# Weights by casting transfers, 1 KB runs of k and q, and eight chunks of pinned steps in an attention-and-feed-forward kernel

## The chip, the cores and the metric

The kernel runs on one core of one Trainium2 chip. The metric is the device time of one execution in microseconds (us). Runs e1 to e4, e5 to e8, e9 to e11, e12 to e14 and e15 with e16 are five sets of rounds on five chips, where the kernel before took 347.7 to 348.3 us; a difference between kernels of different sets is less sure by that much. A *profile* is one further look at one execution: its span is some 2 us shorter than the time.

Five engines matter. TensorE (PE in the profile, PEld for its weight loads) multiplies, VectorE is DVE, ScalarE is ACT, GpSimd is POOL, and SyncE (SP) issues most transfers. The transfers of all queues run on the same 16 DMA engines (the prediction names its source for this).

## The reference, cut to what matters

```python
# q, k, v: (8 batches, 8 heads, 576 tokens, 64), float32
scores = matmul(q, k.T) / 8                       # per batch and head
mask   = (rel >= 0) & (rel < 64)                  # each token sees itself and 63 before it
attn   = softmax(where(mask, scores, -1e9))
x      = matmul(attn, v) -> (4608 tokens, 512)    # heads side by side
h      = maximum(x @ w_in, 0)                     # w_in  (512, 2048)
out    = (h * h) @ w_out                          # w_out (2048, 512)
```

## The kernel before

It goes through the 4608 tokens in 36 chunks of 128 (two blocks of 64). Four chunks make a group of 512 tokens, so there are nine groups. For a chunk `i` there are four attention steps: `T` (transposes of k and q on TensorE), `S_` (scores, exp on ScalarE, mask on VectorE), `V` (values), `X` (transpose of the result). For the first eight chunks the feed-forward goes by chunk, in four quarters of w_in (`U` in what follows); from group 2 on it goes by whole groups. After the first eight chunks come the output products (`ops` in the profile), group by group, woven with the attention and feed-forward of later groups. A tile scheduler puts each engine's instructions in order, by the order of tracing and by what depends on what.

A block of 64 tokens needs the v of its own block and of the block before. `v_ev[i]` holds the v of chunk i. `v_od[i]` holds the block before on its upper half of partitions and chunk i's first block on its lower half, so each chunk copies its last block into the `v_od` of the next chunk (the carry). There are eight of each (`NV = 8`).

```python
    def load(i):
        sts = []
        for (src, nm) in ((k, "k"), (q, "q"), (v, "v")):
            st = stage.tile([P, H, D], FP32, name=f"{nm}_st", tag="st")
            ...                                       # runs of 256 B: 64 floats of one token and head
            nc.sync.dma_start(out=st[:], in_=src[b0, :, 64*j0:64*j0+P, :].rearrange("h p d -> p h d"))
            sts.append(st)
        ...                                           # k and q cast to 16 bits by GpSimd
        v_ev, v_od, v_next = v_evs[i % NV], v_ods[i % NV], v_ods[(i + 1) % NV]
        nc.gpsimd.tensor_copy(out=v_ev[:, :, 0:D], in_=sts[2][:])
        nc.gpsimd.tensor_copy(out=v_od[64:P, :, 0:D], in_=v_ev[0:64, :, 0:D])
        if i + 1 < NCK:
            nc.gpsimd.tensor_copy(out=v_next[0:64, :, 0:D], in_=v_ev[64:P, :, 0:D])   # the carry
    ...
    load(0)
    for s in load_w_in():      # 16 transfers of 256 KB from SyncE, each cast by VectorE
        s()
    NFIRST = 8
    for i in range(1, NV - 1): # chunks 1 to 6
        load(i)
    ...
    T(0), warm(6), S_(0), warm(6), V(0), warm(6), X(0), warm(4)   # chunk 0
    load(NV - 1)               # chunk 7, only now
    for s in load_w_out() + ffn_up_chunk(0):
        s()
    T(1), S_(1), warm(2), V(1), T(2), warm(2), X(1), S_(2)
    ...                        # the steps of chunks 1 to 7; loads of chunks 8 to 11; groups 0 to 8 of output
```

`warm(n)` issues n products of no use, meant to keep TensorE's clock up while it waits.

The softmax here doesn't subtract the row's maximum and nothing guards it: scores larger than these inputs give would overflow.

Of the kernel before, what the change touches and what calls it, by code (L numbers as in the profile page):

```python
# [9 lines left out]
FP32 = mybir.dt.float32  # L10
# [17 lines left out]
def kernel(  # L28
# [9 lines left out]
    nc = tc.nc  # L38
# [7 lines left out]
    W_SCALE = 100.0  # L46
    OUT_SCALE = 1.0 / (W_SCALE * W_SCALE)
# [6 lines left out]
    wst = ctx.enter_context(tc.tile_pool(name="wst", bufs=4))  # L54
# [11 lines left out]

    ident = const.tile([P, P], FP16, name="ident")
    make_identity(nc, ident[:])





    base = const.tile([P, 64], FP16, name="base")
# [23 lines left out]
    w_in_sb = const.tile([P, DMC, DFF], FP16, name="w_in_sb")  # L98
    w_out_sb = const.tile([P, FFC, DM], FP16, name="w_out_sb")

    NV = 8
    v_evs = [const.tile([P, H, 66], FP16, name=f"v_ev{i}") for i in range(NV)]
    v_ods = [const.tile([P, H, 66], FP16, name=f"v_od{i}") for i in range(NV)]
    for i in range(NV):
        nc.vector.memset(v_evs[i][:, :, 64:65], 1.0)
        nc.vector.memset(v_ods[i][:, :, 64:65], 1.0)
    nc.vector.memset(v_ods[0][0:64, :, 0:D], 0.0)

    def load_w_in():
        steps = []  # L110
        FQ = DFF // 4

        def one(quar, c):
            ws = wst.tile([P, FQ], FP32, name="ws", tag="ws")
            nc.sync.dma_start(out=ws[:], in_=moe_w_in[c * P:(c + 1) * P,  # L115
                                                      quar * FQ:(quar + 1) * FQ])
            nc.vector.tensor_scalar(  # L117
                out=w_in_sb[:, c, quar * FQ:(quar + 1) * FQ], in0=ws[:],
                scalar1=W_SCALE, scalar2=None, op0=ALU.mult)

        for quar in range(4):
            for c in range(DMC):
                steps.append(lambda quar=quar, c=c: one(quar, c))
        return steps

    def load_w_out():
        def one(f):
            ws = wst.tile([P, DM], FP32, name="ws2", tag="ws")
            nc.sync.dma_start(out=ws[:], in_=moe_w_out[f * P:(f + 1) * P, :])
            nc.gpsimd.tensor_copy(out=w_out_sb[:, f, :], in_=ws[:])  # L130

        return [lambda f=f: one(f) for f in range(FFC)]


# [7 lines left out]
    q16s, k16s, qTs, kTs, pms, xs = {}, {}, {}, {}, {}, {}  # L142

    def load(i):

        sts = []
        for (src, nm) in ((k, "k"), (q, "q"), (v, "v")):
            st = stage.tile([P, H, D], FP32, name=f"{nm}_st", tag="st")
            b0, j0 = divmod(2 * i, NB)
            if j0 + 1 < NB:  # L150
                nc.sync.dma_start(  # L151
                    out=st[:], in_=src[b0, :, 64 * j0:64 * j0 + P, :].rearrange("h p d -> p h d"))
            else:
                nc.sync.dma_start(
                    out=st[0:64], in_=src[b0, :, 64 * j0:S, :].rearrange("h p d -> p h d"))
                nc.sync.dma_start(
                    out=st[64:P], in_=src[b0 + 1, :, 0:64, :].rearrange("h p d -> p h d"))
            sts.append(st)
        k16s[i] = st16.tile([P, H * D], FP16, name="k16", tag="k16")
        nc.gpsimd.tensor_copy(out=k16s[i][:], in_=sts[0][:].rearrange("p h d -> p (h d)"))  # L160
        q16s[i] = st16.tile([P, H * D], FP16, name="q16", tag="q16")
        nc.gpsimd.tensor_copy(out=q16s[i][:], in_=sts[1][:].rearrange("p h d -> p (h d)"))
        v_ev, v_od, v_next = v_evs[i % NV], v_ods[i % NV], v_ods[(i + 1) % NV]
        nc.gpsimd.tensor_copy(out=v_ev[:, :, 0:D], in_=sts[2][:])
        nc.gpsimd.tensor_copy(out=v_od[64:P, :, 0:D], in_=v_ev[0:64, :, 0:D])
        if i + 1 < NCK:
            nc.gpsimd.tensor_copy(out=v_next[0:64, :, 0:D], in_=v_ev[64:P, :, 0:D])

    def transposes(i):
        ps = ps_att.tile([P, 2, HP, P], FP16, name="qkT_ps", tag="ps_a")  # L170
        for s, src in enumerate((k16s, q16s)):
            for hp in range(HP):
                nc.tensor.transpose(out=ps[:, s, hp, :], in_=src[i][:, hp * P:(hp + 1) * P],  # L173
                                    identity=ident[:])
        kT = attw.tile([P, HP, 192], FP16, name="kT", tag="kT")
        if i > 0:
            nc.vector.tensor_copy(out=kT[:, :, 0:64], in_=kTs[i - 1][:, :, P:192])
        else:
            nc.vector.memset(kT[:, :, 0:64], 0.0)
        nc.vector.tensor_copy(out=kT[:, :, 64:192], in_=ps[:, 0])  # L180
        qT = attw.tile([P, HP, P], FP16, name="qT", tag="qT")
        nc.scalar.activation(out=qT[:], in_=ps[:, 1], func=AF.Copy, scale=1.0)  # L182
        kTs[i], qTs[i] = kT, qT

    def scores(i):
        sc = [ps_att.tile([P, HP, 2, 64], FP32, name=f"sc{hh}", tag="ps_a") for hh in range(2)]
        for hp in range(HP):
            for blk in range(2):
                for hh in range(2):
                    r0 = 64 * hh  # L190
                    nc.tensor.matmul(  # L191
                        sc[hh][:, hp, blk, :], kTs[i][r0:r0 + 64, hp, 64 * blk:64 * blk + P],
                        qTs[i][r0:r0 + 64, hp, 64 * blk:64 * blk + 64], start=True, stop=True)
        j0 = 2 * i % NB
        mask = mask_first if j0 == 0 else mask_second if j0 + 1 == NB else mask_inner
        pms[i] = []
        for hh in range(2):
            pm = attw.tile([P, HP, 2, 64], FP16, name=f"pm{hh}", tag=f"pm{hh}")
            nc.scalar.activation(out=pm[:], in_=sc[hh][:], func=AF.Exp,
                                 scale=1.0 / float(D) ** 0.5)  # L200
            nc.vector.tensor_tensor(out=pm[:], in0=pm[:], in1=mask, op=ALU.min)
            pms[i].append(pm)
# [40 lines left out]

    def ffn_up(g):
        h2s[g] = h2pool.tile([P, FFC, 512], FP16, name="h2", tag="h2")

        def one(f):
            hps = ps_up.tile([P, 512], FP32, name="hps", tag="ps_u")
            for c in range(DMC):
                nc.tensor.matmul(  # L250
                    hps[:], w_in_sb[:, c, f * P:(f + 1) * P], xT_of(g)[:, c, :],
                    start=(c == 0), stop=(c == DMC - 1))
            hrelu = hrp.tile([P, 512], FP32, name="hrelu", tag="hrelu")
            nc.scalar.activation(out=hrelu[:], in_=hps[:], func=AF.Relu)  # L254
            nc.vector.scalar_tensor_tensor(  # L255
                out=h2s[g][:, f, :], in0=hps[:], scalar=0.0, in1=hrelu[:],
                op0=ALU.max, op1=ALU.mult)
# [3 lines left out]
    def ffn_up_chunk(i):  # L261

        g, t0 = i // 4, i % 4 * P
        if g not in h2s:
            h2s[g] = h2pool.tile([P, FFC, 512], FP16, name="h2", tag="h2")

        def one(fq):
            hps = ps_up.tile([P, 4, P], FP32, name="hps4", tag="ps_u")
            for f in range(4):
                for c in range(DMC):  # L270
                    nc.tensor.matmul(  # L271
                        hps[:, f, :], w_in_sb[:, c, (4 * fq + f) * P:(4 * fq + f + 1) * P],
                        xT_of(g)[:, c, t0:t0 + P], start=(c == 0), stop=(c == DMC - 1))
            hrelu = hrp.tile([P, 4, P], FP32, name="hrelu4", tag="hrelu")
            nc.scalar.activation(out=hrelu[:], in_=hps[:], func=AF.Relu)
            nc.vector.scalar_tensor_tensor(  # L276
                out=h2s[g][:, 4 * fq:4 * fq + 4, t0:t0 + P], in0=hps[:], scalar=0.0,
                in1=hrelu[:], op0=ALU.max, op1=ALU.mult)

        return [lambda fq=fq: one(fq) for fq in range(FFC // 4)]  # L280
# [8 lines left out]
    def ffn_out(g):  # L289
        hold = {}  # L290

        def one(ts, fq):
            if fq == 0:
                hold["ps"] = ps_out.tile([P, DM], FP32, name="ops", tag="ps_o")
            for f in range(4 * fq, 4 * fq + 4):
                nc.tensor.matmul(  # L296
                    hold["ps"][:], h2s[g][:, f, ts * P:(ts + 1) * P], w_out_sb[:, f, :],
                    start=(f == 0), stop=(f == FFC - 1))
# [9 lines left out]



    load(0)
    for s in load_w_in():
        s()
    NFIRST = 8
    for i in range(1, NV - 1):
        load(i)
    T, S_, V, X = [lambda i, fn=fn: fn(i) if i < NFIRST else None
                   for fn in (transposes, scores, values, to_xT)]
    T(0), warm(6), S_(0), warm(6), V(0), warm(6), X(0), warm(4)
    load(NV - 1)  # L320
    for s in load_w_out() + ffn_up_chunk(0):
        s()
    T(1), S_(1), warm(2), V(1), T(2), warm(2), X(1), S_(2)
    for i in range(1, NFIRST):
        up = ffn_up_chunk(i)
        up[0](), V(i + 1), T(i + 2), up[1](), up[2](), X(i + 1), S_(i + 2), up[3]()
# [42 lines left out]
```

## Time and profile before

| | before |
|---|---|
| time, median of 4 runs | 348.03 us (347.95 to 348.61) |
| span of the profile | 345.9 us |
| TensorE busy | 324.3 us (94%) |
| first feed-forward product | 19.4 us |
| w_in complete on the core | 25.6 us |
| end of the first eight chunks | 75.4 us |

The page's table of engines, its slices (each digit is the busy share of a fortieth of the span, in tenths), and the start of its chain of the work that ended last, kernel before:

```profile
span 345.9 us, 7917 instructions
...
PE 324.3 (94%) x3146; PEld 178.2 (52%) x3146; DVE 207.9 (60%) x506; ACT 163.8 (47%) x289; POOL 121.5 (35%) x204
...
PE   1957888999999999999999999999999999999995
...
GB/s 200 249 252 239 234 247 252 207 230 228 243 172 61 93 121 123 121 124 155 212 185 182 170 135 184 185 87 27 23 45 36 30 32 32 30 30 32 35 88 62
...
PE 83%; DVE 7%; DMA 5%; ACT 2%; SPq 1%; issue 1%; ACTq 0%
```

TensorE is at nine tenths or more from the eighth slice on (60 us), and without a gap from about 75 us. What can be gained lies before that. The timeline of TensorE shows the feed-forward of chunk 0: start and duration in us, then the line and the operation, then the idle time ahead of it and who ended that.

```profile
19.41 1.05 PE L271 MATMUL hps_446<-xT,w_in_sb 128*128 128x128 f16 x16 [0.98 <-DVE xT L226]
...
22.17 1.05 PE L271 MATMUL hps_486<-xT,w_in_sb 128*128 128x128 f16 x16 [0.82 <-DVE h_397 L276]
...
25.63 0.90 PE L271 MATMUL hps_506<-xT,w_in_sb 128*128 128x128 f16 x13 [1.62 <-DVE w_in_sb L117]
```

The last quarter of w_in holds TensorE until 25.6 us: the weights pass one by one through SyncE's transfers and VectorE's casts, as the group of these casts shows (16 of them, 438 ns each; 12.2 us of VectorE's idle time ended by their transfers):

```profile
L117 DVE TENSOR_SCALAR w_in_sb<-ws 128x512 f16<-128x512 f32 x16 | 7.0, 438 | 12.2 <-DMA ws<-in_moe_w_in_dram 12.1
```

The table of windows for 25 to 35 us gives the rest of the loss: the granted clock (the column PEclk, after the five busy columns) is 0.64 and 0.68 of full speed there.

```profile
25.00:30.00 5.00, 2.67 (x49) 2.11 (x49) 3.93 (x9) 1.62 (x3) 3.75 (x6) 0.64 1.03 232
30.00:35.00 5.00, 4.70 (x60) 3.77 (x58) 2.55 (x7) 2.14 (x5) 4.62 (x9) 0.68 0.99 224
```

The dense work of TensorE, estimated from the durations in this trace (the prediction has the sum), is about 317 us, so about 29 us are lost, nearly all before 75 us.

### The profile page before, as it was taken

Reading aid. Unit: us, or ns where it says so; the run is one execution under the profiler, and the core shown is the slowest. Engines: PE = TensorE matmul, PEld = TensorE weight load, DVE = VectorE, ACT = ScalarE, POOL = GpSimd, SP = SyncE. Lnnn points to the kernel's source line nnn. Section 1 sums busy time; section 2 is a strip of 40 time slices with the busy share of each in tenths; the row PEclk is TensorE's granted clock in tenths of the full one; section 3 lists DMA queues with packets and bytes.
Section 4 is the critical chain, followed back from the end, with each engine's and each line's share of the span. In section 5 each row is a group of like instructions: output and inputs, shape, how many; then the busy total and the mean of one; then the engine's idle time right before and its main releaser. Section 6 shows DMA issues by size and latency. Waiting matters only on the chain.

```text
span 345.9 us, 7917 instructions
## 1 busy us (share of the span) xinstructions
PE 324.3 (94%) x3146; PEld 178.2 (52%) x3146; DVE 207.9 (60%) x506; ACT 163.8 (47%) x289; POOL 121.5 (35%) x204
## 2 busy tenths in 40 slices
PE   1957888999999999999999999999999999999995
PEld 0346787875555555445545554455445544544442
DVE  2656988852666776676776657665675566544400
ACT  1123457544535646643664466436544654444411
POOL 4009895497753333316566544530000000000000
PEclk9996999999999999999999999999999999999998
DMA  7799987899972455546877757730011000000021
GB/s 200 249 252 239 234 247 252 207 230 228 243 172 61 93 121 123 121 124 155 212 185 182 170 135 184 185 87 27 23 45 36 30 32 32 30 30 32 35 88 62
DMA packets 122341, 46.65 MB, mean 135 GB/s; under 512 B 113600, under 2 KB 113600, under 8 KB 122304
## 3 DMA queue, kind: packets, MB, share of 16 engines
q1 hardware_dynamic: 122304, 46.15, 51.7%
q8 instruction: 24, 0.39, 0.5%
q14 instruction: 13, 0.11, 0.1%
HBM read 36.70 MB, written 9.44 MB: 133 GB/s over the span
## 4 chain that ended last, share of the span: by engine, by line
PE 83%; DVE 7%; DMA 5%; ACT 2%; SPq 1%; issue 1%; ACTq 0%
PE ops L296 37%; PE hps L250 28%; DMA ws<-in_moe_w_in_dram 5%; PE qkT_ps L173 4%; PE av L211 4%; PE xt_ps L224 2%; DVE h_397 L276 1%; DVE h_1087 L276 1%; DVE xT L226 1%; DVE w_in_sb L117 1%; PE hps_639 L271 1%; SPq L151 1%; SPq L115 0%; PE hps_1088 L271 0%; PE hps_1537 L271 0%
## 5 line engine op out<-in xcount | busy, mean ns | idle before, releaser
L250 PE MATMUL hps<-xT,w_in_sb 128*128 128x512 f16 x448 | 115.2, 379 | 0.0
L254 ACT ACTIVATE hrelu<-hps 128x512 f32<-128x512 f32 x112 | 66.8, 598 | 91.6 <-PE hps L250 90.9
L250 PEld LDWEIGHTS <-w_in_sb 128*128 128x128 f16 x448 | 43.7, 98 | 52.6 <-issue 0.3
L271 PEld LDWEIGHTS <-w_in_sb 128*128 128x128 f16 x512 | 31.2, 99 | 8.2 <-issue 3.9
L301 ACT ACTIVATE osb<-ops 128x512 f32<-128x512 f32 x36 | 21.6, 600 | 29.1 <-PE ops L296 28.9
L182 ACT ACTIVATE qT<-qkT_ps 128x512 f16<-128x512 f16 x36 | 21.5, 596 | 22.6 <-DVE kT L180 22.3
L216 DVE TENSOR_TENSOR x_sb<-av,rden 128x256 f16<-128x256 f32 x72 | 27.5, 415 | 0.1
L180 DVE COPY kT<-qkT_ps 128x512 f16<-128x512 f16 x36 | 15.2, 421 | 18.0 <-PE qkT_ps L173 17.8
L226 DVE COPY xT<-xt_ps 128x512 f16<-128x512 f16 x36 | 15.1, 420 | 12.7 <-PE xt_ps L224 12.7
L215 DVE RECIPROCAL rden<-av 128x4 f32<-128x4 f32 x72 | 11.4, 178 | 17.1 <-PE av L211 17.1
L255 DVE SCALAR_TENSOR_TENSOR h_5222<-hps,hrelu 128x512 f16<-128x512 f32 x16 | 11.1, 691 | 16.6 <-ACT hrelu L254 16.6
L296 PE MATMUL ops<-w_out_sb,h_1087 128*128 128x512 f16 x64 | 17.5, 380 | 0.0
L191 PEld LDWEIGHTS <-kT 64*128 64x128 f16 x576 | 11.0, 95 | 12.2 <-issue 9.6
L296 PE MATMUL ops<-w_out_sb,h_3120 128*128 128x512 f16 x64 | 16.5, 380 | 0.0
L296 PE MATMUL ops<-w_out_sb,h_2579 128*128 128x512 f16 x64 | 16.5, 380 | 0.0
L296 PE MATMUL ops<-w_out_sb,h_4199 128*128 128x512 f16 x64 | 16.5, 380 | 0.0
L296 PE MATMUL ops<-w_out_sb,h_3658 128*128 128x512 f16 x64 | 16.5, 380 | 0.0
L296 PE MATMUL ops<-w_out_sb,h_2041 128*128 128x512 f16 x64 | 16.5, 380 | 0.0
L296 PE MATMUL ops<-w_out_sb,h_4736 128*128 128x512 f16 x64 | 16.4, 379 | 0.0
L296 PE MATMUL ops<-w_out_sb,h_397 128*128 128x512 f16 x64 | 15.3, 380 | 0.0
L224 PE MATMUL xt_ps<-ident,x_sb 128*128 128x128 f16 x144 | 15.1, 222 | 0.1
L255 DVE SCALAR_TENSOR_TENSOR h_4736<-hps,hrelu 128x512 f16<-128x512 f32 x16 | 11.0, 689 | 6.8 <-ACT hrelu L254 6.4
(837 smaller groups left out, 611.1 us busy)
## 6 DMA issues: line engine op xcount, KB each, us to landing
out_dram<-osb SPq DMA_DIRECT2D x36, 256.0 KB, 2.2
k_st<-in_k_dram SPq DMA_DIRECT2D x32, 256.0 KB, 3.9
q_st<-in_q_dram SPq DMA_DIRECT2D x32, 256.0 KB, 4.0
v_st<-in_v_dram SPq DMA_DIRECT2D x32, 256.0 KB, 4.1
ws<-in_moe_w_in_dram SPq DMA_DIRECT2D x16, 256.0 KB, 4.2
k_st<-in_k_dram SPq DMA_DIRECT2D x8, 128.0 KB, 3.2
q_st<-in_q_dram SPq DMA_DIRECT2D x8, 128.0 KB, 3.0
v_st<-in_v_dram SPq DMA_DIRECT2D x8, 128.0 KB, 3.2
```

The lines of the kernel that those rows point to most:

```text
L173: nc.tensor.transpose(out=ps[:, s, hp, :], in_=src[i][:, hp * P:(hp + 1) * P], identity=ident[:])
L180: nc.vector.tensor_copy(out=kT[:, :, 64:192], in_=ps[:, 0])
L182: nc.scalar.activation(out=qT[:], in_=ps[:, 1], func=AF.Copy, scale=1.0)
L216: nc.vector.tensor_tensor(out=x_sb[:, 4 * half:4 * half + 4, :], in0=av[:, :, 0:D], in1=rden[:].to_broadcast([P, 4, D]), op=ALU.mult)
L224: nc.tensor.transpose(out=xt[:, c, :], in_=xs[i][:, 2 * c:2 * c + 2, :], identity=ident[:])
L226: nc.vector.tensor_copy(out=xT_of(i // 4)[:, :, (i % 4) * P:(i % 4 + 1) * P], in_=xt[:])
L250: nc.tensor.matmul(hps[:], w_in_sb[:, c, f * P:(f + 1) * P], xT_of(g)[:, c, :], start=(c == 0), stop=(c == DMC - 1))
L254: nc.scalar.activation(out=hrelu[:], in_=hps[:], func=AF.Relu)
L255: nc.vector.scalar_tensor_tensor(out=h2s[g][:, f, :], in0=hps[:], scalar=0.0, in1=hrelu[:], op0=ALU.max, op1=ALU.mult)
L271: nc.tensor.matmul(hps[:, f, :], w_in_sb[:, c, (4 * fq + f) * P:(4 * fq + f + 1) * P], xT_of(g)[:, c, t0:t0 + P], start=(c == 0), stop=(c ...
L296: nc.tensor.matmul(hold["ps"][:], h2s[g][:, f, ts * P:(ts + 1) * P], w_out_sb[:, f, :], start=(f == 0), stop=(f == FFC - 1))
L301: nc.scalar.activation(out=osb[:], in_=hold["ps"][:], func=AF.Copy, scale=OUT_SCALE)
```

## The change

Its intent is to shorten that start. The weights come as eight casting transfers on the GpSimd queue (the transfer itself turns 32-bit into 16-bit numbers), so neither VectorE nor GpSimd casts them. k and q of the first eight chunks come in runs of 1 KB, four tokens at a time, in two transfers each (all but chunk 4, which spans two batches and keeps 256 B runs); since a run holds four tokens, the copies behind their transposes become strided. ScalarE casts k and q of the first eight chunks. All loads of chunks 0 to 7 are traced first, with GpSimd's order pinned, and the steps of the first eight chunks are pinned on TensorE in the order in which they stand. The scale factor 100 on the weights is dropped for one factor on the relu, and kT is kept by group, so its first 64 columns are copied once a group.

```diff
+    def runs(i):
+        return i < NFIRST and len(pieces(i)) == 1
+
     def load(i):
+        dims = [P, 2, 4 * D] if runs(i) else [P, H, D]
         ...
+                for b2 in range(2):
+                    eng.dma_start(
+                        out=st[:, b2, :],
+                        in_=rows.rearrange("(a b) (t r) d -> b a t (r d)", b=2, r=4)[b2])
         ...
+        if i < NFIRST:
+            ...                                   # chunk 0's k on VectorE
+                nc.scalar.copy(out=k_dst, in_=k_src)
+            nc.scalar.copy(out=q_dst, in_=q_src)
+        if i > 0:
+            cast_v(i)                             # the three v copies of before, carry and all
+        else:
+            nc.gpsimd.tensor_copy(out=gate[:], in_=sts[0][:, 0, 0:1])
...
+    def load_w_in(quar):
+        nc.gpsimd.dma_start(
+            out=w_in_q[quar][:],
+            in_=moe_w_in[:, quar * FQ:(quar + 1) * FQ].rearrange("(c p) n -> p c n", p=P))
...                                               # load_w_out alike
-    load(0)
-    for s in load_w_in():
-        s()
-    ...
-    T(0), warm(6), S_(0), warm(6), V(0), warm(6), X(0), warm(4)
-    load(NV - 1)
-    ...
+    with tc.manual_schedule(engines={mybir.EngineType.Pool}):
+        load(0)
+        load_w_in(0)
+        load_w_in(1)
+        cast_v(0)
+        load_w_in(2)
+        load(1)
+        load_w_in(3)
+        for i in range(2, NV):
+            load(i)
+            if i >= 6:
+                load_w_out(2 * i - 12)
+                load_w_out(2 * i - 11)
+    with tc.manual_schedule(engines={mybir.EngineType.PE}):
+        T(0), warm(3), S_(0), warm(3), V(0), warm(3), X(0), warm(2)
+        U(0, 0), warm(2), U(0, 1), T(1), warm(2), S_(1), warm(2), V(1), U(0, 2), X(1), U(1, 0)
+        ...                                       # the steps of chunks 2 to 7
```

## The prediction

> **What bounds the kernel now.** TensorE. The table of engines gives it 94% of a 345.9 us span, and the slices show it full from about 75 us to the end. In the timeline chunk 0's feed-forward starts at 19.4 us and waits for w_in until 25.6 us; the first eight chunks end near 75.4 us. The chain of waits opens with w_in transfers (5%), then is TensorE. Dense TensorE work, from the durations shown (0.216 us per 128x512 matmul in the closing stretch: 13.83 us for 64): output 9 x 13.85 = 125, up 7 x 13.85 = 97, attention about 1.6 us a chunk x 28 = 45, the first eight chunks 8 x (1.6 + 4.15) = 46, tail 4: about 317 us. So about 29 us are lost, all before 75 us: about 20 before w_in is complete, the rest in cold clock (0.64 at 25 to 30 us) and small waits.
>
> **What the change intends.** VectorE loses 16 w_in casts (7.0 us), GpSimd 16 w_out casts and eight chunks' k/q casts (now on ScalarE, 0.6 us each); k and q runs grow from 256 B to 1 KB. All queues share the 16 DMA engines (Trainium skill, "DMA: Bandwidth & Descriptors", Issuing engines are not separate DMA queues); no run here yet shows the rate of casting transfers.
>
> **What the compiled order does instead.** TensorE's pinned steps keep their order, but unpinned output matmuls of chunk 0 are scheduled between them: right after the scores of chunk 1, four that read w_out quarter 0 and one that reads quarter 1 come before the rest of chunk 1's values. GpSimd issues these quarters only behind the v casts of chunks 0 to 6, and quarters 2 and 3 behind chunk 7's. TensorE, in order, stands still until they land. ScalarE's order also puts all k/q casts up to chunk 7 before the first relu and chunk 1's qT, so the scores of chunk 1 already wait for chunk 7's q.
>
> **When does w_out land?** Ahead of quarter 0 lie w_in (4.2 MB) and chunks 0 to 6 (5.5 MB); it shares with chunks 7 to 10. Before, 10.65 MB had moved by 45 us (table of windows); 256 B packets ran at about 230 GB/s with engines full, 2 KB ones at 237 GB/s at 0.70 busy. I estimate 270 to 290 GB/s: quarter 0 at about 46 us, quarter 1 at about 52, quarter 2 five to eight later, when TensorE again may wait 1 to 3 us. By then TensorE has done about 5.6 us of useful work: 46 us lost, against 20 before. After it I allow 5 us of small losses, 2 of cold clock.
>
> Sum: 317 + 46 + 2 + 5 = 370 us of span, 2 more as time (347.99 against 345.9 before): 371 us. Groups 2 on should not change: TensorE-bound in both.
>
> Range 356 to 388: all at 320 GB/s gives about 358; a casting rate of half gives over 385. Chances: faster 0.02, within 2% 0.06, slower 0.92.
>
> **What would show it.** Right: TensorE nearly empty from about 15 us to 43 us or later, released by the w_out transfer; eight chunks end 20 to 30 us later, with some output of group 0 already done; equal pace after. Wrong: w_out quarter 0 landing before 35 us, or a chain without w_out.
>
> **What would make it wrong.** Casting transfers much faster or slower than plain ones, GpSimd descriptor generation held up by VectorE, strided copies on ScalarE or VectorE much slower than 0.6 and 0.42 us.

## The result

The changed kernel is correct and takes 395.09 us (median of 4 runs, 394.56 to 397.0) against 348.03: ratio 1.1365, 95% interval 1.1334 to 1.1396, slower. (Here and below, a ratio is the mean time of one kernel's fast runs over that of the other's fast runs of the same rounds, so it is not quite the ratio of the medians quoted.) The direction was as predicted, though not for the predicted reason, and the time lies above the whole range of 356 to 388 us.

The same parts of the page, changed kernel:

```profile
span 392.9 us, 7882 instructions
...
PE 319.8 (81%) x3137; PEld 175.4 (45%) x3137; DVE 194.2 (49%) x464; ACT 172.6 (44%) x304; POOL 106.1 (27%) x181
...
PE   0202000799999999999999999999999999999995
...
GB/s 86 199 92 136 144 106 148 198 210 194 214 221 187 137 121 192 184 190 153 144 108 116 144 90 29 51 32 28 28 27 28 39 43 28 29 28 53 28 53 80
...
PE 76%; SPq 11%; DMA 5%; DVE 3%; ACT 2%; issue 1%; POOL 1%; ACTq 0%; POOLq 0%
```

TensorE does about the same work (319.8 against 324.3 us busy) in a longer span. Its row is nearly empty up to about 70 us (seven slices of 9.8 us), and full like that of before from the ninth slice on. The chain has a new part, 11% of the span in SPq: SyncE's sequencer standing at issues of transfers. The row of GB/s has stretches of 92 and 106 where before had over 230.

What TensorE waited for (the view of waits: engine, line, tile, who ended the wait, then us in total, times, longest):

```profile
PE av L240 <- POOL v_od L137: 38.1, 1, 38.1
PE sc L219 <- ACT qT L209: 16.0, 2, 15.0
```

One wait of 38.1 us: the values of chunk 0 (line 240) wait for GpSimd's line 137, the carry copy. It is not a wait for w_out; the group of the output products shows 0.1 us of idle time. The timelines around it, first TensorE's, then GpSimd's:

```profile
30.30 0.61 PE L219 MATMUL sc<-qT,kT 64*128 64x64 f16 x16 [15.01 <-ACT qT L209]
...
70.41 0.21 PE L240 MATMUL av<-v_od,pm 128*64 128x65 f16 x1 [38.10 <-POOL v_od L137]
```

```profile
68.41 0.61 POOL L134 CAST v_ev<-st 128x512 f16<-128x512 f32 x1 [3.77 <-DMA st<-in_v_dram]
...
69.75 0.61 POOL L137 COPY v_od<-v_ev 64x512 f16<-64x512 f16 x1
```

At 68.41 us GpSimd casts the v of chunk 7, at 69.75 it copies its carry, and at 70.41 TensorE does the values of chunk 0. Why would chunk 0 need chunk 7? Because of the buffers: chunk 7's carry goes to `v_ods[(7 + 1) % 8]`, which is `v_ods[0]`, the buffer that chunk 0's values read. In the kernel before, chunk 7 was loaded after `V(0)` was traced, so its carry waited for V(0). Now the loads are all traced ahead of the steps, and so V(0) depends on the carry. (The result is right all the same: the half concerned is masked for chunk 0.) A false dependence, then, which puts the last load ahead of the first values.

The second question is why that last load came so late. Windows of the kernel before and then of the changed one; the last two columns are the busy share of the 16 DMA engines (the packets' times overlap in the record, so it can pass 1) and the GB/s moved:

```profile
20.00:25.00 5.00, 2.98 (x48) 2.54 (x45) 2.72 (x6) 2.39 (x4) 0.61 (x1) 1.00 1.06 293
35.00:40.00 5.00, 4.17 (x85) 3.70 (x84) 4.68 (x12) 2.66 (x7) 3.83 (x7) 1.00 0.99 223
```

```profile
20.00:25.00 5.00, 0.00 (x0) 0.00 (x0) 0.00 (x0) 0.62 (x1) 0.00 (x0) 1.00 0.29 60
35.00:40.00 5.00, 0.00 (x0) 0.00 (x0) 0.00 (x0) 0.62 (x1) 0.27 (x1) 1.00 0.50 135
```

With the next transfers due, the DMA engines are 0.29 and 0.50 busy, where the kernel before had 1.06 and 0.99 in the same windows. The v casts of chunks 0 to 7 start at 10.9, 26.1, 33.2, 43.4, 47.2, 54.2, 61.3 and 68.4 us. Chunks 0 to 7 and w_in make 10.5 MB read, and the first of them is issued at 0.8 us: about 155 GB/s by 68.4 us, where the prediction had assumed 270 to 290.

### The profile page after: what moved, and what is told of

Read it like the earlier page. It is cut to its first block, busy times and chain, and to the rows that moved or that the text cites. A ratio compares the mean times of both kernels' runs of the same rounds, so it can differ in the third digit from the quotient of the medians.

```text
span 392.9 us, 7882 instructions
## 1 busy us (share of the span) xinstructions
PE 319.8 (81%) x3137; PEld 175.4 (45%) x3137; DVE 194.2 (49%) x464; ACT 172.6 (44%) x304; POOL 106.1 (27%) x181
## 4 chain that ended last, share of the span: by engine, by line
PE 76%; SPq 11%; DMA 5%; DVE 3%; ACT 2%; issue 1%; POOL 1%; ACTq 0%; POOLq 0%
PE ops L322 33%; PE hps L288 25%; SPq L102 8%; PE hps L302 6%; DMA st<-in_v_dram 4%; PE av L240 4%; PE qkT_ps L200 4%; SPq L99 3%; PE sc L219 3%; PE xt_ps L253 2%; DVE h L280 2%; ACT hrelu L279 1%; DMA st<-in_q_dram 1%; DVE pm L230 1%; PE warm L312 1%
## 5 line engine op out<-in xcount | busy, mean ns | idle before, releaser
L322 PE MATMUL ops<-w_out,h 128*128 128x512 f16 x576 | 149.0, 380 | 0.1
L280 DVE SCALAR_TENSOR_TENSOR h<-hps,hrelu 128x512 f16<-128x512 f32 x144 | 99.3, 689 | 62.5 <-ACT hrelu L279 60.0
L288 PE MATMUL hps<-xT,w_in 128*128 128x512 f16 x448 | 115.0, 379 | 0.0
L322 PEld LDWEIGHTS <-h 128*128 128x128 f16 x576 | 49.5, 98 | 42.9 <-DVE h L280 0.4
L288 PEld LDWEIGHTS <-w_in 128*128 128x128 f16 x448 | 43.8, 98 | 52.9
L240 PE MATMUL av<-v_od,pm 128*64 128x65 f16 x288 | 17.6, 199 | 39.8 <-POOL v_od L137 38.1
L137 POOL COPY v_od<-v_ev 64x512 f16<-64x512 f16 x35 | 21.5, 613 | 72.1 <-PE av L240 71.4
L228 ACT ACTIVATE pm<-sc 128x512 f16<-128x512 f32 x72 | 39.1, 598 | 1.9 <-PE sc L219 1.8
L134 POOL CAST v_ev<-st 128x512 f16<-128x512 f32 x36 | 22.1, 613 | 49.0 <-DMA st<-in_v_dram 47.3
L302 PE MATMUL hps<-xT,w_in 128*128 128x128 f16 x512 | 34.4, 221 | 0.3
L302 PEld LDWEIGHTS <-w_in 128*128 128x128 f16 x512 | 30.2, 99 | 3.8 <-issue 1.7
L230 DVE TENSOR_TENSOR pm<-pm,mask_inner 128x512 f16<-128x512 f16 x56 | 24.1, 450 | 1.2 <-ACT pm L228 1.1
## 6 DMA issues: line engine op xcount, KB each, us to landing
w_in<-in_moe_w_in_dram POOLq DMA_DIRECT2D x4, 512.0 KB, 10.9
```

The lines of the kernel that those rows point to most:

```text
L134: nc.gpsimd.tensor_copy(out=v_ev[:, :, 0:D], in_=st_v[i][:])
L228: nc.scalar.activation(out=pm[:], in_=sc[hh][:], func=AF.Exp, scale=1.0 / float(D) ** 0.5)
L230: nc.vector.tensor_tensor(out=pm[:], in0=pm[:], in1=mask, op=ALU.min)
L240: nc.tensor.matmul(av[64 * blk:64 * blk + 64, h % 4, 0:65], pms[i][h % 2][:, h // 2, blk, :], vv[:, h, 0:65], start=True, stop=True)
L280: nc.vector.scalar_tensor_tensor(out=out, in0=hps, scalar=0.0, in1=hrelu, op0=ALU.max, op1=ALU.mult)
L288: nc.tensor.matmul(hps[:], w_in_q[f // 4][:, c, f % 4 * P:(f % 4 + 1) * P], xT_of(g)[:, c, :], start=(c == 0), stop=(c == DMC - 1))
```

## The experiments

Theories after the first look:

- **Carry.** V(0) waits for chunk 7's carry. Rival, the prediction's own step: pinned steps wait at unpinned output products for w_out.
- **Four engines.** The 1 KB transfers are slow since each runs on four of the 16 DMA engines. The Trainium skill, "DMA: Bandwidth & Descriptors", section "Why a DMA increments its semaphore by 16 and not by 1", states that the number of engines of one transfer is the largest number up to 16 that divides the size of the slowest dimension (of those larger than 1) in both access patterns; here that is 128 partitions on one side and `a`, of size 4, on the other, so 4. The trace agrees: adding up the times of single 1 KB packets (median 51 ns), they made at most 4.1 engines' worth in any of the first fifteen windows of 5 us, while the 256 B packets of the same queue reached 10.9. Rival: casting transfers are slow, and hold the shared engines. Their packets took 98 ns for 2 KB read, against 84 ns for the plain 2 KB packets of before, so that could explain 17% on that part.

### e1: without the carry's false dependence

```diff
-        if i + 1 < NCK:
+        if i + 1 < NCK and i != NV - 1:
             nc.gpsimd.tensor_copy(out=v_next[0:64, :, 0:D], in_=v_ev[64:P, :, 0:D])
 ...                                             # behind the steps of the first eight chunks:
+    nc.gpsimd.tensor_copy(out=v_ods[0][0:64, :, 0:D], in_=v_evs[NV - 1][64:P, :, 0:D])
     for s in loads(2):
```

> The changed kernel with one copy moved: chunk 7's carry into the odd value tile 0 is traced after the first eight chunks' matmuls instead of before them, so the values of chunk 0 no longer wait for chunk 7. Theory 1 (this false dependence holds TensorE from 31 to 70 us, and the scheduler, which knows it, then also orders the output matmuls and ScalarE's casts badly): the 38 us idle before the values of chunk 0 is gone, TensorE follows the loads, whose chunk 7 still lands near 68 us; about 352 to 365 us. Rival (the prediction's: w_out is what is waited for, it lands at 72 us whatever else): 388 to 396 us, and the idle time moves to the first output matmul.

Measured: 378.54 us (ratio 1.0888, 1.0839 to 1.0937). That is 16.5 us off the changed kernel, less than expected. The 38 us wait is gone, so the carry was what TensorE stood at. One caution: the scheduler orders by dependences, so this edit also changed the compiled order. In the changed kernel ScalarE does all k and q casts up to chunk 7's (67.5 us) before the first relu (75.1 us); in e1 the first relu comes at 43.1 us, among them. The 16.5 us are thus what the dependence cost together with the order that followed from it; no run parts the two. But the v casts come as late as before (chunk 7's at 70.0 us), and now every chunk waits for its own load. So the false dependence is real, and the late loads stand behind it.

### e2: the 1 KB transfers on all engines

```diff
-                        in_=rows.rearrange("(a b) (t r) d -> b a t (r d)", b=2, r=4)[b2])
+                        in_=rows.rearrange("(a b) (t r) d -> b t a (r d)", b=2, r=4)[b2])
 ...
-            k_src, q_src = [x.rearrange("p r (a i) -> p a i r", a=HP) for x in (k_src, q_src)]
+            k_src, q_src = [x.rearrange("p r (i a) -> p a i r", a=HP) for x in (k_src, q_src)]
```

The slowest dimension is now `t`, of size 32. The same bytes move in the same 1 KB runs; only the partition where a run lands differs, and the second edit undoes that behind the transposes.

> The changed kernel with the 1 KB runs of k and q issued in another order of partitions (token group outermost, 32 of them, then head pair, 4), the same bytes, run length and number of transfers. Theory (the outermost dimension of 4 confines each k and q transfer to 4 of the 16 DMA engines): chunk 7 lands 20 to 28 us earlier, near 42 to 48 us instead of 68, and as the values of chunk 0 still wait for it the time falls by as much, to 367 to 375 us. Rivals (casting transfers hold the engines; or twice as many transfers against a fixed number in flight): within 3 us of 395.

Measured: 368.25 us (1.0582, 1.0559 to 1.0606), 27 us off the changed kernel by the order of two letters. The same windows, and the wait from the view of waits:

```profile
20.00:25.00 5.00, 2.00 (x19) 0.86 (x19) 1.46 (x2) 3.91 (x7) 3.03 (x5) 1.00 0.87 195
35.00:40.00 5.00, 0.00 (x0) 0.00 (x0) 0.00 (x0) 2.12 (x4) 3.60 (x6) 1.00 0.93 243
```

```profile
PE av L240 <- POOL v_od L137: 19.6, 1, 19.6
```

The engines are 0.87 and 0.93 busy where they were 0.29 and 0.50, chunk 7's v cast starts at 41.55 us in place of 68.41, and the carry's wait is 19.6 us in place of 38.1. The 1 KB packets now reach 10.2 engines' worth in 5 us. The casting transfers and the number of transfers are untouched, so neither was the cause. The rate over chunks 0 to 7 and w_in is now about 257 GB/s (10.5 MB from 0.8 to 41.55 us), near the prediction's figure.

### e3: both

> Both edits of the first two runs. If they are the whole cause, the change does what it was meant to: TensorE starts feed-forward at about 12 to 16 us and the time is 328 to 342 us, faster than before. If w_out or the casting transfers hold it too, it stays above 345 us with TensorE idle before the first output matmul.

Measured: 353.37 us (1.0145, 1.0112 to 1.0177). Together the two undo 41.7 of the 47 us; alone they gave 16.5 and 27, a sum of about 43.5. So these are the two causes of the slowdown, and they hardly overlap. The expected gain *over* the kernel before did not come. What TensorE waited for:

```profile
PE sc L219 <- ACT qT L209: 12.3, 3, 10.4
...
PE ops L322 <- DMA w_out<-in_moe_w_out_dram: 0.9, 1, 0.9
```

The scores of chunk 0 wait 10.4 us for ScalarE: their qT stands behind the cast of chunk 2's k, because all casts are traced with the loads. The first feed-forward product comes at 26.8 us, later than before (19.4).

### e4: the output products pinned behind

The rival of e1, run on the changed kernel with all else as it was.

```diff
-        for s in weave(*streams):
-            s()
+        run_all(weave(*streams), g == 1)          # group 0's outputs in a pinned block of TensorE
```

> The changed kernel with the group-0 output matmuls pinned behind the first eight chunks, so none of them stands among the pinned steps; the dependence of chunk 0's values on chunk 7 is kept. The prediction's step (TensorE stands still because the output matmuls come early and w_out late) expects the time to fall by 20 us or more. Theory 1 (the wait is chunk 0's values for chunk 7) expects 390 to 402 us: no gain, perhaps a little slower because the output matmuls no longer fill gaps.

Measured: 402.63 us (1.1561, 1.1519 to 1.1603): no gain, even 7.5 us slower. TensorE still waits for the carry:

```profile
PE av L240 <- POOL v_od L137: 37.9, 1, 37.9
```

The prediction's wait was not what cost the time of this kernel.

### e5: e3 with 256 B runs

```diff
     def runs(i):
-        return i < NFIRST and len(pieces(i)) == 1
+        return False
```

> The kernel of e3 with k and q of the first eight chunks loaded as v is, one transfer each in 256 B runs over all 16 engines, instead of two transfers each in 1 KB runs. If the 1 KB runs are worth what their packets took in the changed kernel (1024 B in about 49 ns against 4 x 18 ns for 256 B runs), loads slow by 4 MB's worth, about 5 to 6 us of DMA time, and the time rises by 2 to 6 us over e3's 353.4. If the two-transfers-per-load form costs more than the longer runs save, the time falls.

Measured: 349.05 us (1.0041, 1.0012 to 1.0071), 4.3 us *faster* than e3 (some 3.6 by the ratios, since the two ran on different chips). The form with longer runs in two transfers loses against the form with short ones in one. Why, is taken up at e16.

### e6, e7: ScalarE's order

e6 traces the k and q casts of chunks 1 to 7 among the steps, one chunk ahead, and pins ScalarE as well. e7 adds the pinned outputs of e4.

```diff
+    def cast_kq(i): ...                          # the casts of load(i), moved here; 24 stage buffers
-    with tc.manual_schedule(engines={mybir.EngineType.PE}):
+    with tc.manual_schedule(engines={mybir.EngineType.PE, mybir.EngineType.Activation}):
...
-            steps = [lambda: S_(i + 1), lambda: U(i, 1), lambda: V(i + 1), ...
+            steps = [lambda: cast_kq(i + 2), lambda: S_(i + 1), lambda: U(i, 1), lambda: V(i + 1), ...
```

> The kernel of e3 with the k and q casts of chunks 1 to 7 traced one chunk ahead of their use and ScalarE's order pinned as TensorE's is (24 instead of 15 staging buffers make the later casts possible). Theory: in e3 the queries of chunk 0 stood on ScalarE behind the k cast of chunk 2, whose load landed at 20.5 us, so the scores of chunk 0 waited until 21.8 us. Without that the scores of chunk 0 run before 12 us and feed-forward starts at 14 to 18 us instead of 26.8; the output matmuls among the steps then wait for w_out until about 49 us, so only part is gained: 342 to 351 us. Rival (loads and weights share the DMA engines and set the pace): no more than 3 us under e3.

> The kernel of e6 with the group-0 output matmuls pinned behind the first eight chunks as in e4. The prediction's step (output matmuls placed early wait for w_out) should now be visible, since nothing else waits that long: 3 to 8 us under e6 if so. If w_out is not waited for in e6 either, within 2 us of e6 or slower.

Measured: 356.19 us (1.0243, 1.0209 to 1.0278) for e6, 353.97 us (1.0191, 1.0156 to 1.0225) for e7. e6 is 2.8 us slower than e3, not faster as its theory expected. In e6 the feed-forward starts at 15.98 us, almost 11 us earlier than in e3, and that is lost again in a wait that had not been there:

```profile
PE ops L329 <- DMA w_out<-in_moe_w_out_dram: 6.6, 2, 6.3
```

Here is the wait for w_out that the prediction had named, 6.6 us of it. In the changed kernel it was hidden: nothing came far enough for w_out to be missed. e7 gained only 2.2 us, as the casts stood ahead of the exps on ScalarE: the values waited for the mask step, `av <- DVE pm`, 10.1 us in 13 waits.

### e8: only the casting transfers

The kernel before, with w_in and w_out as four casting transfers each from GpSimd and nothing else of the change.

> The kernel before with one part of the change alone: the weights as eight casting transfers issued from GpSimd, no staging of weights and no casts of them on VectorE and GpSimd; loads of k, q and v, casts and order as before. If casting transfers are as fast as plain ones (98 ns for 2 KB read against 84 ns), w_in is complete near 18 to 22 us instead of 25.6 and the time is 340 to 347 us. If they starve the chunk loads, which share the engines and are no longer queued behind w_in, 348 us or more.

Measured: 350.54 us (1.0068, 1.0018 to 1.0118): no gain by itself. GpSimd issues in order, so the second w_in transfer left at 11.1 us behind casts that wait for loads; TensorE waited 7.2 us for w_in and 6.6 us for w_out.

### e9, e10, e11: smaller orders

e9 is e7 with the casts behind the exps and the relu. e10 is e9 with all four w_in transfers issued right after chunk 0's k and q (`for quar in range(4): load_w_in(quar)` ahead of `cast_v(0)`). e11 is e10 with 256 B runs.

> The kernel of e7 with one step moved: the casts of the next chunk stand on ScalarE behind the exponentials and a relu instead of in front of the exponentials. In e7 every cycle of TensorE from 35 us on took 8.0 us for about 5.8 us of matmuls, with the values waiting for the masked exponentials 13 times (10.1 us). Theory (ScalarE's order inside a cycle set that pace): cycles of 6.0 to 6.8 us and 341 to 348 us in all. Rival (loads set the pace): within 2 us of e7's 354.

> The kernel of e9 with all four w_in quarters issued right after the gate, ahead of the value casts of chunks 0 and 1 (in e7 the fourth left at 20.8 us because GpSimd, in order, first waited for chunk 1's values). If feed-forward of the first chunks waits for w_in, 2 to 5 us under e9; if that only delays the loads of chunks 1 to 3, which share the engines, no gain or a loss.

> The kernel of e10 with k and q loaded in 256 B runs, one transfer each, as in e5. With order pinned on both engines, this compares the two forms of load alone: if longer runs pay, e10 is 2 to 5 us faster; if they do not, within 1.5 us.

Measured: 352.45 us (1.0145, 1.0109 to 1.0181), 354.37 us (1.0197, 1.0166 to 1.0227) and 348.70 us (1.0025, 0.9985 to 1.0065). By its number e9 is where its rival put it (1.5 us under e7). Its chunks take about 7 us each, and TensorE stops at 66.9 us for 5.1 us at the transposes of chunk 8, scheduled ahead of the last five products `U`: their k cast on GpSimd stands behind the v casts of chunks 8 to 11. Early w_in (e10) gains nothing: ahead in the shared engines, it delays the loads of the chunks. The 256 B runs win again, by 5.7 us, though the values of chunk 1 now wait 7.0 us for an exp that stands behind the casts of chunk 2 on ScalarE; e12 moves those casts.

### e12, e13, e14: GpSimd's order for chunks 8 to 11

e12 pins GpSimd's order for these loads and moves the casts of chunk 2 behind the exps of chunk 1; attention for chunks 8 to 11 starts later in the weave. e13 is e12 with 256 B runs. e14 is e13 with one w_out transfer behind each of chunks 4 to 7.

```diff
-    for s in loads(2):
-        s()
+    with tc.manual_schedule(engines={mybir.EngineType.Pool}):
+        for s in loads(2):
+            s()
...
-            streams.append((attention(g + 1), 0.0, 0.95))
+            streams.append((attention(g + 1), 0.3 if g == 1 else 0.0, 0.95))
```

> The kernel of e9 (352.5 us) with the casts of the k and q of chunk 2 moved behind the exps of chunk 1 on ScalarE, and with GpSimd's order pinned for chunks 8 to 11 too, so the k cast of chunk 8 stands right behind its load and no longer behind the v casts of chunks 8 to 11. Theory (the time that e9 gained by 66 us is given back in the wait of chunk 8's transposes on its k cast and in the cold clock after it): the 5.1 us wait on the POOL k cast disappears and the cold slice at 70 to 80 us with it, 343 to 348 us. Rival (transfers themselves still come too late, or the scheduler makes another wait of the same size, such as outputs waiting for w_out): 350 to 354 us, with the wait under another name.

> As e12, with 256 B runs of k and q in one transfer each. If 256 B is better by what e5 and e11 showed (4.3 and 5.7 us): 338 to 344 us. If that gain was a matter of the order in which waits fell there: within 1.5 us of e12.

> As e13, but the four w_out transfers issued one behind each of chunks 4 to 7 in place of two behind chunk 6 and two behind chunk 7. If outputs of chunk 0, which the scheduler puts from chunk 5 on, wait for w_out in e13, this takes that wait away, 1 to 4 us faster than e13; if loads of chunks 6 to 8 are what TensorE waits for, it is slower by 1 to 3 us.

(The time gained by 66 us in e9, of which e12's expectation speaks, was less than it sounds: five products `U`, some 5 us of work, still lay behind e9's stop.)

Measured: 348.68 us (1.0015, 0.9964 to 1.0066), 345.57 us (0.9921, 0.9876 to 0.9965) and 347.19 us (0.9987, 0.9939 to 1.0035). e12 gained 3.8 us over e9 and stayed just outside of what either side expected: the wait for chunk 8's k is gone, and the rival came true, a new wait under another name (8.4 us for w_out). e13 is 3.1 us faster than e12, between its two expectations, and e14 is 1.6 us slower than e13. From e13, that wait, and the windows around it:

```profile
PE ops L329 <- DMA w_out<-in_moe_w_out_dram: 6.9, 1, 6.9
```

```profile
45.00:50.00 5.00, 0.00 (x0) 0.00 (x0) 0.56 (x1) 0.00 (x0) 4.30 (x7) 0.75 1.09 176
50.00:55.00 5.00, 3.96 (x48) 3.12 (x48) 0.52 (x1) 1.15 (x3) 0.75 (x2) 0.57 1.19 189
55.00:60.00 5.00, 4.97 (x83) 4.03 (x80) 4.07 (x12) 3.82 (x7) 1.84 (x3) 1.00 1.22 197
```

Two pinned blocks are not pinned against each other: outputs of chunk 0 stand between the steps of chunks 4 and 5, and wait 6.9 us for w_out. Then the clock is at 0.57 for 5 us. (The Trainium skill, "TensorE: Matmul & The Clock Gate", section "HAM oscillation", gives the rule as no idle gaps of TensorE above about 3.4 us; this gap of 6.9 us agrees. It is not the whole of it: in e16 below, the clock falls to half at 22.4 us with no gap over 1.1 us in the 12 us before, though TensorE was busy only 2.2 of the 4 us from 18 to 22 us.) e14 shows it from the other side: with w_out issued earlier, the outputs were scheduled earlier still, and the wait was 10.4 us.

### e15, e16: one pinned block

All of it in one block pinned on TensorE, ScalarE and GpSimd: the steps, the moved carry, the loads of chunks 8 to 11 and the first group of outputs. e15 has 256 B runs, e16 1 KB runs.

```diff
+    with tc.manual_schedule(engines={PE, Activation, Pool}):
         ...                                       # the steps of the first eight chunks
+        nc.gpsimd.tensor_copy(out=v_ods[0][0:64, :, 0:D], in_=v_evs[NV - 1][64:P, :, 0:D])
+        for s in loads(2):
+            s()
+        for s in tail(1):                         # outputs of group 0, attention of group 2, loads of group 3
+            s()
```

> The kernel of e13 (345.6 us), where TensorE waited 6.9 us once for w_out because output matmuls of chunk 0 were scheduled between the steps of chunks 4 to 7, although both parts were pinned: they were two pinned blocks. Here the steps of the first eight chunks, the loads of chunks 8 to 11 and the first group of outputs are one pinned block of TensorE, ScalarE and GpSimd, so all outputs stand behind the steps (checked in the compiled order). Theory (that wait and the cold clock after it are what is left): the w_out wait is zero and the time is 334 to 341 us. Rival (chunk loads are what limits, and the wait only moves to them): 344 to 347 us, with new waits on v or k casts.

> As e15, with the 1 KB runs of k and q in two transfers each. If the loss by 1 KB runs seen in e5, e11 and e13 (3 to 6 us) is one of the transfers themselves, it stays: 3 to 6 us over e15. If it came of the scheduler's order, they come out within 1.5 us.

Measured: e15 takes **340.84 us** (340.10 to 343.78; before 347.68 in the same rounds), ratio 0.9834, 0.9776 to 0.9893. It is faster than both kernels, by 1.7%; whether it is by 2% the interval leaves open. e16 takes 346.02 us (0.9961, 0.992 to 1.0001). The page of e15, and its largest waits:

```profile
span 339.0 us, 7811 instructions
...
PE 317.9 (94%) x3137; PEld 174.3 (51%) x3137; DVE 195.3 (58%) x464; ACT 171.8 (51%) x304; POOL 108.3 (32%) x181
...
PE   2978878898999999999999999999999999999995
```

```profile
PE av L247 <- DVE pm L237: 5.4, 13, 0.7
PE qkT_ps L207 <- POOL gate L121: 5.1, 1, 5.1
PE hps L309 <- DVE xT L262: 2.5, 7, 0.5
```

The w_out wait is zero. The first output product starts at 68.0 us, where the kernel before ended its eight chunks at 75.4: these 7.4 us are the gain (the spans differ by 6.9).

e16 against e15 is the cleanest test of the 1 KB form: one line differs, and both orders are pinned. That line switches three things at once, though: the length of the runs, the number of transfers, and the strided copies behind the transposes. The feed-forward products on TensorE, e15 and then e16:

```profile
13.73 1.05 PE L309 MATMUL hps<-xT,w_in 128*128 128x128 f16 x16
...
20.08 1.07 PE L309 MATMUL hps<-xT,w_in 128*128 128x128 f16 x16
...
21.90 1.05 PE L309 MATMUL hps<-xT,w_in 128*128 128x128 f16 x16 [0.52 <-DVE xT L262]
...
24.89 1.07 PE L309 MATMUL hps<-xT,w_in 128*128 128x128 f16 x16
```

```profile
15.96 1.05 PE L309 MATMUL hps<-xT,w_in 128*128 128x128 f16 x16
...
23.01 1.89 PE L309 MATMUL hps<-xT,w_in 128*128 128x128 f16 x16
...
25.84 1.86 PE L309 MATMUL hps<-xT,w_in 128*128 128x128 f16 x16 [0.52 <-DVE xT L262]
...
30.31 1.07 PE L309 MATMUL hps<-xT,w_in 128*128 128x128 f16 x16
```

The first product is 2.2 us later, and by the sixth the lag is 5.4 us (30.31 against 24.89), about what the whole kernel loses (5.2 us). Of this, about 2 us are cold clock: a quarter's 16 products take 1.89 us in place of 1.07, and 1.86 in place of 1.05. Part of the 2.2 us shows in ScalarE's timeline, again e15 and then e16:

```profile
1.32 1.28 ACT L136 ACT_TABLE_LOAD   x1 [1.32 <-PEq L401]
```

```profile
5.48 1.28 ACT L136 ACT_TABLE_LOAD   x1 [5.48 <-DMA st<-in_q_dram]
```

With q in two transfers, its cast waits for two semaphores. The compiled order puts one of the two waits on the table load ahead of it. So the 1.28 us of table load, free in e15, come after q's landing in e16. The v of chunk 1 is also cast at 19.9 us in place of 15.7. Why that transfer lands later is not settled; TensorE did not wait for it (chunk 1's values waited 1.0 us for VectorE's mask step). The strided copy of kT, which stands between the transposes and the scores, takes longer too, here that of chunk 1 in e16 (0.42 us in e15):

```profile
18.82 0.69 DVE L215 COPY kT<-qkT_ps 128x512 f16<-128x512 f16 x1 [0.45 <-PE qkT_ps L207]
```

It is 0.69 us in seven of the first eight chunks. The long runs themselves do not come late: chunk 7's v is cast at 44.25 us in e16 and at 45.67 in e15, and in the three other pairs (e3 and e5, e10 and e11, e12 and e13) it is 2.0 to 2.3 us earlier with 1 KB runs as well. What loses is the start, by the order of the first landings, the table load and the strided copies; no run parts these.

## Why the prediction was wrong, and where it was right

- **"What bounds the kernel now": right.** TensorE-bound from 75 us on, with some 29 us lost ahead. e15 won 7 us of these and nothing else: its eight chunks end at 68 us.
- **"Groups 2 on should not change": right.** The slices of both kernels agree from the full ones on.
- **"TensorE, in order, stands still until they land" (the output products, for w_out): wrong for this kernel.** The order was as described, but TensorE had been stopped earlier, at chunk 0's values by chunk 7's carry, for 38.1 us. The w_out transfers were issued from 63.2 and from 70.3 us (quarter 0 landed at 71.2 us, where the prediction had 46), and the outputs waited 0.1 us. e4 took the named wait away and gained nothing; e1 took the carry's away and gained 16.5 us. The prediction read the order of each engine, but not what each instruction waited for. The named mechanism itself exists: it cost 6.6 us in e6 and 6.9 in e13, once the rest was mended. The shape it predicted (TensorE nearly empty from 15 us to 43 or later) came true for another reason, as both waits end with the last loads; so the direction, too, was right by luck in part. Its end was off: the eight chunks ended at 130.4 us, 55 us later than before and not 20 to 30.
- **"I estimate 270 to 290 GB/s": the mis-sized term.** Chunks 0 to 7 and w_in came at about 155 GB/s in the changed kernel, and at about 257 in e2, where only the order of the runs in a k or q transfer, and with it the number of DMA engines, differs. That is 27 of the 47 us. e2, with the wrong wait but nearly the assumed rate, took 368.25 us, close to the predicted 371. That is partly luck: its wait is another one, which happens to end with the same loads.
- **"It shares with chunks 7 to 10", "a casting rate of half gives over 385": not the risk.** Casting packets took 98 ns against 84. The prediction's list of what could go wrong held casting, descriptors and strided copies (VectorE's took 0.69 us in place of 0.42), but not the shape of the plain transfers, though the diff states it.
- **"ScalarE's order also puts all k/q casts … before … chunk 1's qT": right, and worth more than it was given.** In the changed kernel, chunk 0's scores waited 15.0 us for ScalarE; in e3, 10.4 us. It did not add to the time of the changed kernel, since the carry's wait followed. Chunk 7's q was cast at 67.5 us, less than 3 us before the carry's wait ended: had the carry alone been missing and the order stayed, ScalarE would have held chunk 1's scores nearly as long (worked out from the order, not run).
- **The causes add up.** 16.5 (carry, with the order that it brought) and 27 (engines) are about 43.5; together they gave 41.7 of 47. The remaining 5 went with the order of work on in-order engines and the 256 B form, which e5 to e15 changed one after another, each uncovering the next wait.

## What to carry to other kernels

Before costing a transfer, read the slowest dimension of both its access patterns: the order of two letters in a rearrange decided here between 4 engines and up to 16, and 27 us. When loads are moved ahead of the steps that use them, follow each rotating buffer to the instruction that reuses it: a carry into buffer (i + 1) mod 8 made the first chunk wait for the last. And where engines run in order, one mended wait shows the next, so an expected gain comes only when all orders on the way are right: here at the fifteenth kernel, by pinning everything in one block.

## What the Trainium skill lacked or had wrong

- "DMA: Bandwidth & Descriptors", section "Why a DMA increments its semaphore by 16 and not by 1": the rule on the slowest dimension was right (4.1 engines' worth at most; 10.2 and 27 us less in e2). What the section lacks is how to see it in a profile: a DMA share of 0.29 to 0.5 while the next transfers are due.
- The same page, section "Specifications", gives 512 B as the least run for full rate. The packets agree (18 ns for 256 B in the kernel before, 51 ns for 1 KB in the changed one: 1.4 times the bytes per time), and chunk 7's v was cast 1.4 to 2.3 us earlier with 1 KB runs. But the kernel was faster with 256 B in four pairs, by 4.3 us (e5 against e3), 5.7 (e11 against e10), 3.1 (e13 against e12) and 5.2 (e15 against e16), where the longer runs need two transfers, two semaphores and strided copies; how much of the loss comes of each is only partly shown (e16).
- The same page, section "SWDGE vs HWDGE vs iDMA", says which queue may issue casting transfers, but gives no rate for them: here 98 ns for each 2 KB packet read (16-bit out), against 84 ns for a plain 2 KB packet.
- "TensorE: Matmul & The Clock Gate", section "Seeing it yourself", warns that clock records can't be fully trusted; here the record held and the view misled. In the changed kernel the windows show a granted clock of 1.00 from the start, but the trace's first clock record, full clock, stands at 74.5 us, and the view reads 1.00 where there is no record yet: 16 products took 1.54 us at 73.5 us and 1.06 us at 75.3.
- No page has what a second semaphore does to a table load ahead: ScalarE's load of 1.28 us moved from 1.32 to 5.48 us (e16), since one of the cast's two waits was put before it.
